# A decode layer on one Trainium2 core: the order of the loads, wo, w1 and w3 in single transfers, K transposed in place, one exp per row

## The chip, the cores and the metric

The kernel runs on one core of one Trainium2 chip. The metric is the device time of one execution in microseconds (us). Inputs and weights lie in HBM in bf16; every weight and the used part of the K and V caches are read once, 55.58 MB in all.

## The reference, cut to what matters

```python
# B=4, Sq=1, D=1024, Hq=32, Hkv=4, Sk=8192, Dh=128, F=3584; W = 2048 (the last keys)
h  = x + attention(layernorm(x))
    # q = layernorm(x) @ wq ; k, v = last W rows of the caches, each shared by 8 heads
    # p = softmax(q k^T * Dh**-0.5) ; attention = (p v) @ wo
h2 = h + (silu(n @ w1) * (n @ w3)) @ w2        # n = layernorm(h)
```

Four tokens, one per batch entry, pass through one attention block and one gated feed-forward block. There is little arithmetic per byte: each weight multiplies four rows.

## The kernel before

The kernel is written as a straight sequence. The scheduler of the framework is switched off (`tc.manual_schedule()`), so each engine executes its instructions in the order in which the code writes them: TensorE (PE) the matmuls and transposes, VectorE (DVE) and ScalarE (ACT) the copies, reductions and the exp, GpSimd (POOL) constants. SyncE (SP) issues all weight and cache loads, in the order of the list `ring` (L106), and an issue that has to wait holds back all that are behind it.

**Loads.** `stream` has five slots of 32 KB per partition. `fill()` (L118) issues the next part of `ring` as soon as the slot used five parts earlier has been given back by `done(...)`. The order is: the first half of wq, K in two pairs of batches, two slots that are reserved for the transposed K (kT, no load), the second half of wq, V in two pairs, wo in two pairs (four loads), w1 in two halves, w3 in two halves, w2 in six pieces of 7, 6, 8, 4, 2 and 1 rows per partition (L107). The pieces shrink so that little work is left after the last landing.

**Attention.** x comes in by four small loads on ACT's queue (L149), is transposed (L225) and normalised (`layernorm_T`, L192). The first half of wq is multiplied (L244, four strips of 32 array columns at once). Then K is transposed by PE in 32 steps of eight 128x128 blocks into PSUM (L264), and DVE and ACT in turn copy each step out to kT (L266, L268). The second half of wq follows, then q is copied, transposed (L278) and placed into Qm (L284). Scores are computed batch by batch (L299). For each batch there is a row maximum (`row_max`, L310), a bias by matmul, four exps (L339), each for one group g of heads: the bias of the other groups' rows is -1e30, so that each exp writes the probabilities of its own group and zeros elsewhere, interleaved by g. DVE transposes the result in 32x32 blocks (`transpose_p`, L349), and `output` (L358) multiplies with V (L374), scales by the inverse row sum and a mask (L383), and adds the four parts (L391). Eight small matmuls (L414), a copy, a DVE transpose and another copy bring the result into the layout oP.

**After attention.** wo is multiplied in 128 matmuls of 256 columns in four strips (L439); x is added by DVE (L449), the second layernorm follows, then w1 (L463), the gate silu (L477 to L481, with a reciprocal of 896 elements), w3, the product (L485), a transpose, and w2 (L496) piece by piece. Four small stores end the kernel.

Of the kernel before, what the change touches and what calls it, by code (L numbers as in the profile page):

```python
# [10 lines left out]
P = 128  # L11
# [6 lines left out]
NSLOT = 5  # L18
SLOT = 16384
NEG = -1.0e30  # L20
# [3 lines left out]
def kernel(  # L24
# [32 lines left out]
    C = 4  # L57
# [12 lines left out]
    T = REP  # L70
    L5 = 8
    JR = W // R
    JB = 8
    JM = 4
    wo_v = A_wo.rearrange("(g p t) n -> p g (t n)", g=Hkv, t=T)
# [8 lines left out]
    stream = ctx.enter_context(tc.tile_pool(name="stream", bufs=NSLOT))  # L84
# [4 lines left out]
    def of_cache(cache, b):  # L89
        return cache[b, :, Sk - W : Sk, :].rearrange("g (i j) d -> i g (j d)", j=JR)  # L90

    def pair(parts):
        return [parts[0:2], parts[2:4]]

    k_, v_ = (
        pair([(name, b, [JR, Dh], of_cache(cache, b)) for b in range(B)])
        for name, cache in (("k", A_k_cache), ("v", A_v_cache))
    )
    kT_ = pair([("kT", b, [JR, P], None) for b in range(B)])
    wo_ = pair([("wo", g, [1, T * D], wo_v[:, g : g + 1, :]) for g in range(Hkv)])  # L100

    def four_rows(name, view, n):
        return [[(name, i, [4, n], view[:, 4 * i : 4 * i + 4, :])] for i in range(KC // 4)]

    wq_ = four_rows("wq", wq_v, NQ)
    ring = wq_[:1] + k_ + kT_ + wq_[1:] + v_ + wo_ + four_rows("w1", w1_v, F) + four_rows("w3", w3_v, F)  # L106
    W2B = [7, 6, 8, 4, 2, 1]  # L107
    w2_ = []
    f0 = 0
    for i, n in enumerate(W2B):  # L110
        w2_.append(("w2", i, [n, D], w2_v[:, f0 : f0 + n, :]))
        f0 += n
    ring += [w2_[:2], w2_[2:]]
    views = {}
    taken = []
    used = set()

    def fill():  # L118

        while len(taken) < len(ring):  # L120
            n = len(taken) - NSLOT
            if n >= 0 and not all((name, i) in used for name, i, _, _ in ring[n]):
                break
            parts = ring[len(taken)]
            slot = stream.tile([P, SLOT], BF16, tag="slot", name="s_" + parts[0][0])
            o = 0
            for name, i, shape, src in parts:
                dst = slot[:, o : o + int(np.prod(shape))]
                o += int(np.prod(shape))
                view = dst.rearrange("p (a b) -> p a b", a=shape[0])  # L130
                if src is not None:
                    nc.sync.dma_start(out=dst if name in ("k", "v") else view, in_=src)  # L132
                views[(name, i)] = view
            taken.append(slot)

    def get(name, i):
        return views[(name, i)]

    def done(name, i):
        used.add((name, i))  # L140
        fill()
# [5 lines left out]
    nc.vector.memset(x_nat[:], 0.0)  # L147
    for c in range(C):
        nc.scalar.dma_start(out=x_nat[R * c : R * c + B, :], in_=x_flat[:, c * DQ : (c + 1) * DQ])  # L149
    fill()  # L150
# [3 lines left out]
    ones_f = const.tile([P, P], FP32)  # L154
    nc.vector.memset(ones_f[:], 1.0)
    eps_t = const.tile([P, 1], FP32)
    nc.vector.memset(eps_t[:], eps)

    t32 = const.tile([P, R], FP32)
    nc.vector.tensor_reduce(  # L160
        out=t32[:], in_=ident[:].rearrange("p (q h) -> p h q", q=C), axis=AX.X, op=ALU.add
    )
    ident_f = const.tile([P, P], FP32)
    nc.gpsimd.tensor_copy(out=ident_f[:], in_=ident[:])
    same = const.tile([P, C, R], FP32)
    for q in range(C):
        nc.gpsimd.tensor_copy(out=same[:, q], in_=t32[:])
    negm = const.tile([P, Hkv], FP32)
    nc.vector.tensor_reduce(
        out=negm[:], in_=t32[:].rearrange("p (g r) -> p g r", g=Hkv), axis=AX.X, op=ALU.add  # L170
    )
    nc.vector.tensor_scalar(
        out=negm[:], in0=negm[:], scalar1=-1.0, scalar2=-NEG, op0=ALU.add, op1=ALU.mult
    )
    jmask = const.tile([P, JM, 1], FP32)
    nc.vector.tensor_reduce(
        out=jmask[:, :, 0], in_=ident[:].rearrange("p (j h) -> p j h", j=JM), axis=AX.X, op=ALU.add
    )
    nscale = const.tile([P, Hkv], FP32)
    nc.vector.memset(nscale[:], -qscale)  # L180

    strip = const.tile([P, 2, P + B - 1], FP32)
    nc.gpsimd.memset(strip[:], 0.0)
    for l in range(2):
        nc.gpsimd.tensor_copy(
            out=strip[:, l, B - 1 :].rearrange("p (c x) -> p c x", c=C)[:, :, : B * Hkv].rearrange(
                "p c (g b) -> p c g b", b=B
            )[:, :, :, 0],
            in_=t32[:].rearrange("p (g c l) -> p l c g", g=Hkv, c=C)[:, l],
        )  # L190

    def layernorm_T(h_T, tag):  # L192

        both = act.tile([P, 2, KC, B], FP32, tag=tag + "_both")
        nc.vector.tensor_copy(out=both[:, 0], in_=h_T[:, :, :B])
        nc.vector.tensor_tensor(out=both[:, 1], in0=both[:, 0], in1=both[:, 0], op=ALU.mult)  # L196
        sums_ps = ps.tile([P, 2, KC, B], FP32, tag="kt3")
        nc.tensor.matmul(sums_ps[:], lhsT=ones_f[:], rhs=both[:], start=True, stop=True)  # L198
        sums = act.tile([P, 2, B], FP32, tag=tag + "_sums")
        nc.vector.tensor_reduce(  # L200
            out=sums[:], in_=sums_ps[:].rearrange("p t k b -> p t b k"), axis=AX.X, op=ALU.add
        )
        mean = act.tile([P, 2, B], FP32, tag=tag + "_mean")
        nc.vector.tensor_single_scalar(out=mean[:], in_=sums[:], scalar=1.0 / D, op=ALU.mult)
        rstd = act.tile([P, 1, B], FP32, tag=tag + "_rstd")
        nc.vector.tensor_tensor(out=rstd[:, 0], in0=mean[:, 0], in1=mean[:, 0], op=ALU.mult)
        nc.vector.tensor_tensor(out=rstd[:, 0], in0=mean[:, 1], in1=rstd[:, 0], op=ALU.subtract)  # L207
        nc.scalar.activation(  # L208
            out=rstd[:, 0], in_=rstd[:, 0], func=ACT.Sqrt, bias=eps_t[:], scale=1.0
        )  # L210
        nc.vector.reciprocal(out=rstd[:, 0], in_=rstd[:, 0])
        n_T = act.tile([P, KC, R], BF16, tag=tag + "_nT")
        nc.gpsimd.memset(n_T[:], 0.0)
        hc = act.tile([P, KC, B], FP32, tag=tag + "_hc")
        nc.vector.tensor_tensor(
            out=hc[:], in0=both[:, 0], in1=mean[:, 0:1, :].to_broadcast([P, KC, B]), op=ALU.subtract
        )
        nc.vector.tensor_tensor(
            out=n_T[:, :, :B], in0=hc[:], in1=rstd[:].to_broadcast([P, KC, B]), op=ALU.mult
        )  # L220
        return n_T
# [7 lines left out]
    x_T = act.tile([P, KC, R], BF16)  # L229
# [4 lines left out]
    q_ps = [ps.tile([P, REP // 2, Dh], FP32, tag=f"sc{hf}", name=f"q_ps{hf}") for hf in range(2)]  # L234
    HALF = REP // 2

    def query(i):
        w = get("wq", i)
        for kk in range(4):
            kc = 4 * i + kk  # L240
            for hf in range(2):
                for c in range(C):
                    o = (2 * c + hf) * HALF * Dh
                    nc.tensor.matmul(  # L244
                        q_ps[hf][R * c : R * c + R],
                        lhsT=xn_T[:, kc, :],
                        rhs=w[:, kk, o : o + HALF * Dh],
                        start=(kc == 0),
                        stop=(kc == KC - 1),
                        tile_position=(0, R * c),  # L250
                    )
        done("wq", i)

    query(0)


    n_step = 0
    for b in range(B):
        k = get("k", b)
        kT = get("kT", b)  # L260
        for jb in range(JR // JB):
            kt_ps = ps.tile([P, JB, P], BF16, tag=f"kt{n_step % 3}")
            for jj in range(JB):
                nc.tensor.transpose(out=kt_ps[:, jj], in_=k[:, jb * JB + jj, :], identity=ident[:])  # L264
            if n_step % 2 == 0:
                nc.vector.tensor_copy(out=kT[:, jb * JB : (jb + 1) * JB], in_=kt_ps[:])  # L266
            else:
                nc.scalar.copy(out=kT[:, jb * JB : (jb + 1) * JB], in_=kt_ps[:])  # L268
            n_step += 1
        done("k", b)  # L270

    query(1)
    q_sb = act.tile([P, REP, Dh], BF16)
    nc.vector.tensor_copy(out=q_sb[:, :HALF], in_=q_ps[0][:])
    nc.scalar.copy(out=q_sb[:, HALF:], in_=q_ps[1][:])
    qT_ps = ps.tile([P, REP, Hkv, R], BF16, tag="kt0")
# [6 lines left out]
    for b in range(B):  # L283
        nc.vector.tensor_copy(  # L284
            out=Qm[:, b].rearrange("p (g y) -> p g y", y=QW)[:, :, :REP],
            in_=qT_ps[:, :, :, b].rearrange("p r g -> p g r"),
        )


    sc_ps = [ps.tile([P, W // C], FP32, tag=f"sc{b}", name=f"sc_ps{b}") for b in range(B)]  # L290
# [4 lines left out]
    def scores(b, gs):  # L295
# [11 lines left out]
        if Hkv - 1 in gs:  # L307
            done("kT", b)
# [234 lines left out]
```

## Time and profile before

| | |
|---|---|
| time, median of 3 runs | 139.3 us (139.28 to 139.4) |
| the profiled execution's own time | 139.33 us |
| its span from the first to the last instruction | 137.5 us |
| mean granted TensorE clock | 0.812 |
| HBM read | 55.58 MB, 404 GB/s over the span |
| instructions | 2022 |

How to read the lines of the profile: a group names its source line, the engine, the operation, the tiles written and read, the shapes (partitions x elements, type) and the count; after the bar come its busy us and the mean ns of one; after the second bar the idle time of that engine just before, and what ended it. PEld is the weight load of TensorE, which overlaps with PE. In the 40 slices each entry stands for 3.44 us. PEclk is the clock that was granted to TensorE as a share of full speed. The chain of waits follows the work that ended last back from the last instruction.

### The profile page before, as it was taken

Reading aid. Unit: us, or ns where it says so; the run is one execution under the profiler, and the core shown is the slowest. Engines: PE = TensorE matmul, PEld = TensorE weight load, DVE = VectorE, ACT = ScalarE, POOL = GpSimd, SP = SyncE. Lnnn points to the kernel's source line nnn. Section 1 sums busy time; section 2 is a strip of 40 time slices with the busy share of each in tenths; the row PEclk is TensorE's granted clock in tenths of the full one; section 3 lists DMA queues with packets and bytes.
Section 4 is the critical chain, followed back from the end, with each engine's and each line's share of the span. In section 5 each row is a group of like instructions: output and inputs, shape, how many; then the busy total and the mean of one; then the engine's idle time right before and its main releaser. Section 6 shows DMA issues by size and latency. Waiting matters only on the chain.

```text
span 137.5 us, 2022 instructions
## 1 busy us (share of the span) xinstructions
PE 78.7 (57%) x866; PEld 45.4 (33%) x868; DVE 52.6 (38%) x97; ACT 42.7 (31%) x57; POOL 4.2 (3%) x18
## 2 busy tenths in 40 slices
PE   0000299999903889328936997948539600834271
PEld 0000139898801422114303353536424300322240
DVE  3001505666700235187165359551330596160001
ACT  1200006989820325998803940000040200000000
POOL 7400000000000000000000000000000000000000
PEclk9999999999995599955595599995995995595555
DMA  5998999999899999999999999999999999999950
GB/s 152 458 459 382 429 434 434 415 438 505 376 410 429 415 438 419 434 429 415 443 417 429 422 467 425 438 417 434 425 430 425 425 447 388 414 437 431 400 219 2
DMA packets 3529, 55.72 MB, mean 405 GB/s; under 512 B 416, under 2 KB 448, under 8 KB 704
## 3 DMA queue, kind: packets, MB, share of 16 engines
q1 hardware_dynamic: 3472, 55.58, 95.2%
q8 instruction: 7, 0.11, 0.3%
q10 hardware_dynamic: 48, 0.01, 0.0%
q14 instruction: 2, 0.02, 0.0%
HBM read 55.58 MB, written 0.01 MB: 404 GB/s over the span
## 4 chain that ended last, share of the span: by engine, by line
DMA 51%; PE 28%; DVE 13%; ACT 4%; issue 2%; SPq 1%; DVEq 0%
DMA s_wq<-in_A_wq_dram 31%; DMA s_w<-in_B_w_dram 20%; PE o_ps L374 11%; ACT P L339 4%; PE y_ps L439 4%; PE sc_ps L299 3%; DVE PT L351 3%; PE q_ps L244 2%; DVE om L391 2%; PE gu_ps L463 2%; DVE od L383 2%; PE tot_ps L360 1%; PE nm_ps L328 1%; PE on_ps L414 1%; SPq L132 1%
## 5 line engine op out<-in xcount | busy, mean ns | idle before, releaser
L339 ACT ACTIVATE P<-sc_ps,bias 128x512 bf16<-128x512 f32 x16 | 19.7, 1421 | 10.8 <-DVE bias L336 10.8
L374 PE MATMUL o_ps<-s_v,PT 128*128 128x512 bf16 x62 | 18.4, 457 | 0.3 <-issue 0.2
L268 ACT COPY s_kT<-kt_ps 128x1024 bf16<-128x1024 bf16 x16 | 15.6, 1012 | 6.8 <-PE kt_ps L264 6.8
L264 PE MATMUL kt_ps<-ident,s_k 128*128 128x128 bf16 x256 | 16.1, 219 | 1.1 <-ACT s_kT L268 1.0
L264 PEld LDWEIGHTS <-s_k 128*128 128x128 bf16 x256 | 15.0, 98 | 2.9 <-issue 2.5
L463 PE MATMUL gu_ps<-s_w,n_T 128*32 128x448 bf16 x128 | 9.8, 474 | 9.8 <-DMA s_w<-in_B_w_dram 8.0
L266 DVE COPY s_kT<-kt_ps 128x1024 bf16<-128x1024 bf16 x16 | 11.1, 692 | 10.1 <-PE kt_ps L264 10.1
L244 PE MATMUL q_ps<-s_wq,n_T 128*32 128x512 bf16 x64 | 7.2, 630 | 7.4 <-DMA s_wq<-in_A_wq_dram 5.6
L496 PE MATMUL y_ps<-s_w,hg_T 128*32 128x256 bf16 x112 | 6.6, 386 | 7.9 <-DMA s_w<-in_B_w_dram 5.3
L374 PEld LDWEIGHTS <-PT 128*128 128x128 bf16 x64 | 7.6, 123 | 9.8 <-issue 5.5
L208 ACT ACTIVATE rstd<-rstd,eps_t 128x4 f32<-128x4 f32 x2 | 0.6, 297 | 32.4 <-DVE rstd L207 32.4
L198 PE MATMUL sums_ps<-both,ones_f 128*128 128x64 f32 x4 | 1.1, 374 | 16.1 <-DVE both L196 16.1
L351 DVE STREAM_TRANSPOSE PT<-P 128x2048 bf16<-128x2048 bf16 x4 | 9.2, 2304 | 2.7 <-ACT P L339 2.7
L463 PEld LDWEIGHTS <-n_T 128*32 128x32 bf16 x128 | 4.4, 122 | 14.5 <-issue 11.5
L299 PE MATMUL sc_ps<-s_kT,Qm 128*32 128x512 bf16 x64 | 8.5, 603 | 0.4 <-DVE Qm L284 0.4
L496 PEld LDWEIGHTS <-hg_T 128*32 128x32 bf16 x112 | 4.2, 124 | 10.8 <-issue 6.8
L383 DVE SCALAR_TENSOR_TENSOR od<-o_ps,rinv,jmask 128x512 f32<-128x512 f32 x4 | 3.0, 750 | 9.4 <-PE o_ps L374 9.3
L198 PEld LDWEIGHTS sums_ps<-both,ones_f 128*128 128x128 f32 x4 | 0.8, 250 | 16.4 <-DVE both L196 16.4
L315 PE MATMUL mx_ps<-ident_f,rmax 128*1 128x128 f32 x8 | 1.9, 333 | 7.4 <-DVE rmax L313 7.4
L244 PEld LDWEIGHTS <-n_T 128*32 128x32 bf16 x64 | 2.4, 139 | 10.8 <-issue 8.6
L479 DVE RECIPROCAL eg<-eg 128x896 f32<-128x896 f32 x1 | 5.8, 5753 | 0.0
L439 PE MATMUL y_ps<-s_wo,oP 128*32 128x256 bf16 x128 | 4.9, 326 | 1.5 <-DVE oP L427 1.5
(68 smaller groups left out, 59.7 us busy)
## 6 DMA issues: line engine op xcount, KB each, us to landing
s_w<-in_B_w_dram SPq DMA_DIRECT2D x4, 3584.0 KB
s_wq<-in_A_wq_dram SPq DMA_DIRECT2D x2, 4096.0 KB, 12.3
s_k<-in_A_k_cache_dram SPq DMA_DIRECT2D x4, 2048.0 KB, 20.5
s_v<-in_A_v_cache_dram SPq DMA_DIRECT2D x4, 2048.0 KB
s_wo<-in_A_wo_dram SPq DMA_DIRECT2D x4, 2048.0 KB, 25.1
s_w<-in_B_w_dram SPq DMA_DIRECT2D x1, 2048.0 KB, 24.7
s_w<-in_B_w_dram SPq DMA_DIRECT2D x1, 1792.0 KB
s_w<-in_B_w_dram SPq DMA_DIRECT2D x1, 1536.0 KB
```

Of the source, the lines that this page charges most:

```text
L244: nc.tensor.matmul(q_ps[hf][R * c : R * c + R], lhsT=xn_T[:, kc, :], rhs=w[:, kk, o : o + HALF * Dh], start=(kc == 0), stop=(kc == KC - 1) ...
L264: nc.tensor.transpose(out=kt_ps[:, jj], in_=k[:, jb * JB + jj, :], identity=ident[:])
L266: nc.vector.tensor_copy(out=kT[:, jb * JB : (jb + 1) * JB], in_=kt_ps[:])
L268: nc.scalar.copy(out=kT[:, jb * JB : (jb + 1) * JB], in_=kt_ps[:])
L299: nc.tensor.matmul(sc_ps[b][R * q : R * q + R], lhsT=Qm[:, b, g * R : (g + 1) * R], rhs=v[:, g, q], start=(g == 0), stop=(g == Hkv - 1), t ...
L339: nc.scalar.activation(out=P4[:, :, :, g], in_=sc_ps[b][:].rearrange("p (j i) -> p j i", i=L5), func=ACT.Exp, bias=bias[:, g : g + 1], sca ...
L351: nc.vector.transpose(out=PT[:].rearrange("p j h -> p (j h)"), in_=stage.pop(("P4", b))[:].rearrange("p j i g -> p (j i g)"),)
L374: nc.tensor.matmul(o_ps[:], lhsT=PT[:, i * JM : (i + 1) * JM, :].rearrange("p j h -> p (j h)"), rhs=v[:, i * JM : (i + 1) * JM, :], start= ...
L439: nc.tensor.matmul(y_ps[R * c : R * c + R, :], lhsT=oP[:, g, t, :], rhs=w[:, 0, o : o + DQ], start=(g == 0 and t == 0), stop=(g == Hkv - 1 ...
L463: nc.tensor.matmul(out_ps[hf][R * c : R * c + R], lhsT=hn_T[:, kc, :], rhs=w[:, kk, o : o + FH], start=(kc == 0), stop=(kc == KC - 1), til ...
L479: nc.vector.reciprocal(out=eg[:], in_=eg[:])
L496: nc.tensor.matmul(y2_ps[R * c : R * c + R, :], lhsT=hg_T[:, fc, :], rhs=w[:, ff, c * DQ : (c + 1) * DQ], start=(fc == 0), stop=(fc == FC ...
```

## The change

- **Loads.** The ring of slots becomes one tile `ring` of five units of 32 KB per partition, and each matrix has a fixed place: wq in units 0 and 1, V of batches 0 and 1 in unit 2, K in units 3 and 4, V of batches 2 and 3 in unit 0, wo in units 3 and 4, w1 from unit 1, w3 from unit 3, w2's first 13 rows in unit 0 and the rest in unit 1. The order is now wq (one row of 8 KB per partition, then seven rows, 56 KB), K, V, wo in one load of 64 KB per partition, w1 and w3 in one load of 56 KB each, w2 in five pieces (13, 8, 4, 2, 1). Each load stands in the code behind the last reader of the place that it fills.
- **K.** A step has 16 blocks instead of 8, and its copy goes back to where the blocks came from (`transpose_k`). The scores of batches 0 and 1 stand between the transposes; those of batches 2 and 3 come after all of them. Batches 0 and 1 have three PSUM buffers for the steps, batches 2 and 3 have two.
- **Softmax.** Maximum and bias are computed for two batches at once. There is one exp per batch, written densely (`softmax`); DVE then multiplies it with a group mask into the interleaved layout (`spread`).
- **Output.** The four parts are added by POOL in two steps; four small matmuls (`place`) and one ACT copy bring the result into oP. x is added to wo's product by four matmuls with the identity, and wo's product itself is 64 matmuls of 512 columns in two strips.
- **Small steps.** Several constants, two steps of the layernorm's variance and its subtraction go from DVE to POOL; its copy and square to ACT; the gate's +1 from DVE to ACT. The products of w1 and w3 each go into one PSUM tile and are read in one instruction each.

The diff's core:

```diff
-    ring = wq_[:1] + k_ + kT_ + wq_[1:] + v_ + wo_ + four_rows("w1", w1_v, F) + four_rows("w3", w3_v, F)
-    W2B = [7, 6, 8, 4, 2, 1]
+    ring = stream.tile([P, 5 * UNIT], BF16)
+    wq_s = at(0, KC, NQ)
+    k_s = at(3, B, JR, Dh)
+    v_s = [at((2, 0)[b // 2], 2, JR, Dh)[:, b % 2] for b in range(B)]
+    wo_s = at(3, T, D)
+    w1_s = at(1, KC, F)
+    w3_s = at(3, KC, F)
+    W2B = [13, 8, 4, 2, 1]
...
+    for r in (slice(0, 1), slice(1, KC)):
+        load(wq_s[:, r, :], wq_v[:, r, :])
+    for b in range(B):
+        load(k_s[:, b].rearrange("p j d -> p (j d)"), k_v[:, :, b])
+    load_values(0)
...
+    load_values(1)                       # behind the query's matmuls
+    nc.scalar.copy(out=q_sb[:], in_=q_ps[:].rearrange("p a r d -> p (a r) d"))
...
+    def transpose_k(b, tags):
+        for n in range(JR // JB):        # JB = 16
+            blocks = k_s[:, b, n * JB : (n + 1) * JB, :]
+            kt_ps = ps.tile([P, JB, P], BF16, tag=tags[n_step % len(tags)], name="kt_ps")
+            for jj in range(JB):
+                nc.tensor.transpose(out=kt_ps[:, jj], in_=blocks[:, jj, :], identity=ident[:])
+            if n_step % 2 == 0:
+                nc.vector.tensor_copy(out=blocks, in_=kt_ps[:])
+            else:
+                nc.scalar.copy(out=blocks, in_=kt_ps[:])
+            n_step += 1
...
+    def spread(b):
+        nc.vector.tensor_tensor(
+            out=P4[:],
+            in0=stage.pop(("p1", b))[:].rearrange("p (x o) -> p x o", o=1).to_broadcast([P, JR * L5, Hkv]),
+            in1=gmask[:].to_broadcast([P, JR * L5, Hkv]),
+            op=ALU.mult,
+        )
...
+    transpose_k(0, ("ktA", "ktB", "scB"))
+    scores_tile(0)
+    scores(0, GS)
+    transpose_k(1, ("ktA", "ktB", "scB"))
+    scores(1, GS)
+    small = ps.tile([P, 2, 512], FP32, tag="ktB")
+    row_max(0)
+    transpose_k(2, ("ktA", "scB"))
+    bias_of(0)
+    softmax(0)
+    softmax(1)
+    spread(0)
+    transpose_k(3, ("ktA", "scB"))
+    scores_tile(1)
+    scores(2, GS)
+    scores(3, GS)
+    load(wo_s, wo_v.rearrange("p (t n) -> p t n", t=T))
+    transpose_p(0)
+    row_max(1)
+    spread(1)
+    bias_of(1)
+    softmax(2)
+    softmax(3)
+    transpose_p(1)
+    total(0)
+    output(0)
+    spread(2)
+    transpose_p(2)
+    output(1)
+    load(w1_s, w1_v)
+    spread(3)
+    transpose_p(3)
+    total(1)
+    output(2)
+    output(3)
...
+    for t in range(T):                   # T = 32
+        row = wo_s[:, t].rearrange("p (k i n) -> p i k n", k=2, i=2)
+        for i in range(2):
+            nc.tensor.matmul(
+                y_ps[R * i : R * i + R], lhsT=oP[:, t, :], rhs=row[:, i],
+                start=False, stop=(t == T - 1), tile_position=(0, R * i), skip_group_check=True,
+            )
+    load(w3_s, w3_v)
+    load(w2_s[0], w2_v[:, : W2B[0], :])
...
+    up_projection(w1_s, gate_ps)
+    for w, n in zip(w2_s[1:], W2B[1:]):
+        load(w, w2_v[:, fc : fc + n, :])
```

## The prediction

> **What bounds the kernel now.** I read the page's engine shares first, then the rate in the 40 slices, then busy time by stage (windows), then the chain of waits.
>
> ```profile
> span 137.5 us, 2022 instructions
> PE 78.7 (57%) x866; PEld 45.4 (33%) x868; DVE 52.6 (38%) x97; ACT 42.7 (31%) x57; POOL 4.2 (3%) x18
> GB/s 152 458 459 382 429 434 434 415 438 505 376 410 429 415 438 419 434 429 415 443 417 429 422 467 425 438 417 434 425 430 425 425 447 388 414 437 431 400 219 2
> q1 hardware_dynamic: 3472, 55.58, 95.2%
> DMA 51%; PE 28%; DVE 13%; ACT 4%; issue 2%; SPq 1%; DVEq 0%
> ```
>
> No engine is busy for more than 57% of the span, but the one load queue is busy for 95%, and no slice between the ramp at the start and the end falls away. The kernel is a stream of 55.58 MB at about 430 GB/s (129.3 us). The first six slices (20.6 us) moved 7.95 MB, which at 430 GB/s takes 18.5 us: the stream acts as if it began at 2.1 us, 1.4 us after its first issue at 0.73. It would end at 131.4; another 6.1 us pass to the end (engines that finish later, the last products, the store). So only two things matter: does a load always stand in the queue, and how long is the tail. The chain's PE and DVE parts are compute that runs beside the stream.
>
> Prices come from these groups and stretches (mean ns after the comma; in the last three rows PE's and DVE's busy us come third and fifth, PEclk and GB/s last):
>
> ```profile
> L268 ACT COPY s_kT<-kt_ps 128x1024 bf16<-128x1024 bf16 x16 | 15.6, 1012 | 6.8 <-PE kt_ps L264 6.8
> L266 DVE COPY s_kT<-kt_ps 128x1024 bf16<-128x1024 bf16 x16 | 11.1, 692 | 10.1 <-PE kt_ps L264 10.1
> L275 ACT CAST q_sb<-q_ps 128x512 bf16<-128x512 f32 x1 | 0.6, 586 | 8.2 <-PE q_ps L244 8.2
> L481 DVE TENSOR_TENSOR eg<-gu_ps,eg 128x448 f32<-128x448 f32 x2 | 1.2, 620 | 0.1
> L351 DVE STREAM_TRANSPOSE PT<-P 128x2048 bf16<-128x2048 bf16 x4 | 9.2, 2304 | 2.7 <-ACT P L339 2.7
> L339 ACT ACT_TABLE_LOAD x1 | 1.3, 1283 | 0.0
> 43.39 3.60 PE L244 MATMUL q_ps<-s_wq,n_T 128*32 128x512 bf16 x32 [5.60 <-DMA s_wq<-in_A_wq_dram]
> 35.79 2.00 PE L264 MATMUL kt_ps<-ident,s_k 128*128 128x128 bf16 x32 [0.16 <-ACT s_kT L268]
> 90.00:92.50 2.50, 1.38 (x10) 1.19 (x10) 0.99 (x3) 0.00 (x0) 0.00 (x0) 1.00 1.03 436
> 92.50:95.00 2.50, 1.58 (x32) 1.20 (x36) 0.77 (x2) 0.00 (x0) 0.00 (x0) 0.51 0.96 413
> 95.00:97.50 2.50, 2.50 (x84) 2.13 (x80) 0.00 (x0) 0.00 (x0) 0.00 (x0) 0.81 1.04 447
> ```
>
> **Part 1, fewer and longer transfers.** The bytes are the same. The trace's packets take 612 ns for 16 KB, 1066 for 28 and 1214 for 32, so each carries about 9 ns besides its bytes. Each of the 16 engines is spared 24 packets of wo, 8 of w1, 8 of w3 and 8 of w2 (six pieces become five): 48 x 9 ns = -0.4 us. 56 and 64 KB packets are not in the trace; between 32 KB's rate and none of this gain, 0 to -0.5. The store, the last load (one w2 row) and its products are the same, so the tail stays.
>
> **Part 2, the deadline that wo gets.** Before, wo took two slots as kT's were released one by one, and its four loads were issued from 47.0 to 53.1 us. Now wo_s covers exactly k_s (units 3 and 4), so its single load waits in SP's queue for the last scores matmul of batch 3. Ahead of it stand wq, K and V, 25.17 MB: 2.1 + 58.5 = 60.7 us. With 1.4 us from issue to rate, wo must be issued by 59.3. Behind it in SP's queue stand w1, w3 and w2, so each us late is a us of empty queue for everybody. The loads ahead of it are safe: V's second half waits for the query products (28.4 below) and is due at 2.1 + 48.8 - 1.4 = 49.5.
>
> **Part 3, when the scores end.** I follow the written order on each engine.
> - wq has landed at 2.1 + 19.5 + 1.2 (the chain has the first wq landing at 13.05, that much after 2.1 + 9.75) = 22.8. The x rows alternate with SP's packets as before, and layernorm takes about 3.6 us after them (13.35 to 17.0 now), so it is ready by then; the constants and three layernorm steps that go to POOL and two that go to ACT cost a few tenths under the same cover. Were all four x loads stuck between 56 KB packets, the cover would be gone and it would be 2 us late.
> - Query: row 0 is done; 14 groups of four remain. 8 groups took 3.60 us at half clock: 6.2 us, some 5.6 if the clock rises underway: 28.4. Then q_sb in one ACT copy (1.0, as for 1024 in L268), eight transposes (1.0), one Qm copy (0.35), handoffs: 30.9. K0's first chunk reuses qT's buffer and waits for it.
> - A chunk is now 16 transposes: 32 took 2.00 with a stop, 56 ns each at full clock, so 0.9, or 1.7 at half. ACT's eviction of 2048: 586 to 1012 ns for 512 to 1024 is 0.83 ns per element, so 1.86; DVE's 1.25 (159 ns + 0.52 per element, from L266 and the fixed part of L481). K0: four chunks 4.5 (first one at half clock), and ACT's second eviction ends 6.6 after the start: 37.5. scores(0) holds PE 1.7 (four groups of 0.43, as now). K1: 5.8 more; scores(1) 1.7 + 0.6 drain: 47.3. These eviction tails were hidden before, since scores came long after the last transpose.
> - row_max(0) stands ahead of K2 in PE's order: a reduce of 1024 (1.2, twice L313's 0.68 less the fixed part), the small matmul 0.4: K2 starts at 49.1. It has two buffers; the ACT one paces: two chunks, eviction, last chunk, eviction: 55.8.
> - ACT then loads the exp table (1.28, at that place in its order), and one exp: a plain 448 took 0.54 and the read of the sum is 0.29, so 0.9 (up to 1.4, L339's): 58.0. spread(0) on DVE, 2048 products: L481 gives 1.04 ns per element, 2.3; L266's bf16 rate would give 1.2. The change puts two broadcast operands in it, nearest to L481: 60.3.
> - K3's first eviction on DVE is queued behind that spread: 61.6. The third and fourth chunks wait for its buffer: 1.8 to 3.4, then ACT's last eviction 1.9, scores(2) and (3) 3.4 + 0.6. **The wo load is issued at about 70** (69.5 to 71).
>
> So the queue is empty for 70 - 59.3 = 10.7 us. Engines that ran ahead of the slowest meet again in that pause (the last slices fall to 219 GB/s over a full slice), worth some 0.5 us at the end.
>
> [...]
>
> The clock rows above: PE fell to half clock at 92.5 with 1.38 us of work in the 2.5 before, in two bursts. By the sums above the K stage has PE at 47 to 75% with pauses of 1 to 2.5 us, so I count half clock for some chunks (1.6 us in K3, 0.9 in K0). [...]
>
> **Part 4, what comes after.** One exp per row saves ACT 12 of 16 (about 1.2 apart: 14 us), all beside the stream. DVE gains four spreads (9.2) and loses the om sums (4.2) to POOL, at 0.3 to 1.1 per add. Both chains wait on DVE: from scores(3) at 70.6, reduce, small matmul, qmax, spread and bias (4.9), output(0) (5), od + spread + transpose for batches 2 and 3 (10.6), output(3) (3.5 to 5), od, adds, on, oP (3): about 99. w1 is issued after output(1) at about 85, and wo lasts until 91: in time. wo's product now uses two of four column strips: 4.9 us before, 32 pairs of 0.216 or 0.427 now, 7 to 13.7; y ends at 106 to 113. w3 waits for it; wo and w1 last until 71.4 + 36.6 = 108, so w3 is due at 106.6: late by 0 to 6. With the first 3.4 us at half clock, as after the gap at 92.5 now, the product takes 8.6: I take 1. The second layernorm, w1's product and the gate (its 5.75 us reciprocal) lie under w3 and the first w2 piece, 25 us of stream; the last four w2 pieces wait for w1's product, at about 118, and are due at 132.
>
> **Sum.** Profiled run 139.33 = span 137.5 + 1.83 around it; the median of the three runs is 139.3. Span: 137.5 - 0.4 + 10.7 - 0.5 + 1 = 148.3, minus 0.6 for the middle of the clock and spread bounds: 147.7; time 149.5.
>
> **Rivals.**
> - *The queue never runs dry* (faster). If scores(3) ends by 59.3, only -0.4 remains: 138.9. For: K has landed by 43, and PE's own work on K and scores is 14.4 + 6.8 us, which from 30.9 ends at 52. It decides at 59.3: 11 us of waits would have to vanish. Against: every wait above follows from an order written out. 5%.
> - *A short stall.* Full clock throughout, spread at the bf16 rate, table load hidden, evictions cheaper by 0.2 each: 70 - 2.5 - 1.1 - 1.3 - 0.5 = 64.6 and up to 1 earlier, so 3.8 to 5.3 us of empty queue on 139.33 - 0.9: 142.2 to 143.7. 10%.
> - *Two stalls.* PE at half clock through K1 to K3 (8 chunks, half of it exposed: +3) and through wo's product (+6): 154 to 158. For: the clock slices show 0.5 after each pause; against: the product follows output(3) directly, and warmed up in 2.5 us at 95. 12%.
> - *Nothing visible*, gain and a small stall cancelling (wo at 60 to 60.5): 2%.
>
> **How the numbers follow.** The forecast case, wo late by 6 to 13 us, holds 71%; with 0 to 2 us for w3 it spans 144 to 153.5. The range 142.5 to 154 adds the near ends of its two neighbours. 0.2% (0.28 us) is about what a measurement can tell: faster 0.05, same 0.02, slower 0.93.
>
> **What would show it.** In the profile after: a hole in GB/s from about 61 to 71 us; SP waiting for PE's scores before wo's issue; a wo product starting on DMA or on output, and y's matmuls at about 7 to 9 us; DVE's eviction of K3's third step right behind a 2.3 us TENSOR_TENSOR; ACT evictions of 1.86. An unbroken stream with wo issued before 59 makes the forecast wrong as a whole; an ACT eviction under 1.5 or full PE clock from 30 to 70 shrinks it.

## The result, and the profile after

The changed kernel takes 152.1 us (median of six runs, 151.25 to 152.66), against 139.42 for the kernel before on the same chip (six runs, 139.28 to 139.51). The ratio is 1.090, 95% interval 1.086 to 1.095: 12.7 us slower. The profiled run is the highest of the six, 152.66 us, with a span of 150.9. The medians and ranges of the experiments are those of fast runs, so one slow run of e2 (153.65 us) and one of e4 (148.58 us) are left out of them.

The page of the kernel after, its engine shares, its rate in 40 slices of 3.77 us, the load queue, and the engines' shares of the chain:

```profile
span 150.9 us, 1801 instructions
PE 75.9 (50%) x786; PEld 42.8 (28%) x788; DVE 48.6 (32%) x45; ACT 28.4 (19%) x31; POOL 15.0 (10%) x39
GB/s 185 581 472 258 487 378 417 421 447 434 426 417 417 421 443 430 52 0 278 278 556 278 556 324 441 476 487 426 289 471 476 395 350 413 424 404 413 319 24 4
q1 hardware_dynamic: 2608, 55.58, 87.0%
PE 33%; DMA 32%; DVE 13%; ACT 11%; issue 5%; POOL 2%; ACTq 0%; POOLq 0%; DVEq 0%
```

The same 55.58 MB are moved, and every engine but POOL is busy for less time than before. But slices 17 and 18 hold 52 and 0 GB/s, the queue's share falls from 95.2 to 87.0%, and the chain now runs through compute: DMA holds 32% of it instead of 51. (The 278s and 556s behind the hole are not a slow stream: a 64 KB packet takes 2.42 us, and its bytes are booked in one slice. The whole stretch from 73 to 107 us gives 432.)

The hole by stretches of 2.5 us (after the length: PE, PEld, DVE, ACT, POOL busy us, PEclk, DMA share, GB/s):

```profile
60.00:62.50 2.50, 2.16 (x21) 2.16 (x21) 0.54 (x2) 0.00 (x0) 0.00 (x0) 0.50 0.37 151
62.50:65.00 2.50, 1.41 (x14) 1.25 (x12) 2.50 (x2) 1.05 (x1) 0.00 (x0) 0.71 0.00 0
65.00:67.50 2.50, 1.63 (x16) 0.49 (x19) 0.69 (x1) 0.82 (x1) 0.00 (x0) 1.00 0.00 0
67.50:70.00 2.50, 1.99 (x20) 0.38 (x12) 0.47 (x1) 0.00 (x0) 0.00 (x0) 1.00 0.00 0
```

Most of the 16 DMA engines finish V's last packets at about 60.9 (two only at 62.3 and 62.7), wo is issued at 69.56 and its packets begin at 70.54: 9.6 us with nothing in the queue for most of them. What ran meanwhile stands in the chain of the kernel after (start, length, what):

```profile
54.76 1.28 ACT L324
...
56.90 2.17 issue
59.07 1.23 DVE ring L262
...
60.34 3.58 PE kt_ps L260 x32
63.95 1.87 ACT ring L264
65.87 3.65 PE sc_ps L283 x27
```

This is the written order, read off: behind ACT's last eviction of K2 come the exp table and the exp; the 2.17 us called issue is DVE in spread(0) (56.86 to 59.16). Only then comes DVE's eviction for K3, two chunks of K3 that had waited for its buffer, ACT's eviction, and the scores of batches 2 and 3. SP's own waits name what each of the late loads stood behind (total us, times, longest):

```profile
SPq L123 <- PE y_ps L460: 14.5, 1, 14.5
SPq L123 <- PE small L374: 11.5, 1, 11.5
...
SPq L123 <- PE sc_ps L283: 6.0, 1, 6.0
```

They are, in this order, w3 behind wo's product (issued at 105.78), w1 behind output(1) (81.49) and wo behind the scores (69.56). Only the last left the whole queue empty: w1's last packets land between 107.7 and 109.6, after w3 is already queued. (By a narrow margin: two engines had finished w1 by 107.84 and got their first packets of w3 only at 109.42 and 109.47; neither is the one whose w3 lands last.) The priced groups:

```profile
L264 ACT COPY ring<-kt_ps 128x2048 bf16<-128x2048 bf16 x8 | 14.8, 1866 | 19.7 <-PE kt_ps L260 19.7
L262 DVE COPY ring<-kt_ps 128x2048 bf16<-128x2048 bf16 x8 | 9.8, 1224 | 11.5 <-PE kt_ps L260 11.5
L337 DVE TENSOR_TENSOR P<-p,gmask 128x2048 bf16<-128x2048 bf16 x4 | 9.1, 2280 | 3.5 <-ACT p L324 3.5
L391 POOL TENSOR_TENSOR o<-od 128x256 f32<-128x256 f32 x4 | 6.8, 1695 | 64.6 <-DVE od L382 64.6
L460 PE MATMUL y_ps<-ring,oP 128*32 128x512 bf16 x64 | 8.8, 443 | 0.1
```

**Where the 13.4 us of span are.** The first DMA engine to finish has its last landing at 142.51 instead of 132.14: +10.4. The last engine follows 3.6 us later instead of 1.9: +1.75. From the last landing to the end it takes 4.7 us instead of 3.5: +1.25. The +10.4 is the 9.6 us of empty queue, plus 0.5 to 1.0 for wo's first packets (2.9 to 3.4 us instead of 2.42), less the spared packets.

### The profile page after: what moved, and what is told of

The parts are those of the page before. It is cut to its first block, busy times and chain, and to the rows that moved or that the text cites. A ratio compares the mean times of both kernels' runs of the same rounds, so it can differ in the third digit from the quotient of the medians.

```text
span 150.9 us, 1801 instructions
## 1 busy us (share of the span) xinstructions
PE 75.9 (50%) x786; PEld 42.8 (28%) x788; DVE 48.6 (32%) x45; ACT 28.4 (19%) x31; POOL 15.0 (10%) x39
## 3 DMA queue, kind: packets, MB, share of 16 engines
q1 hardware_dynamic: 2608, 55.58, 87.0%
HBM read 55.58 MB, written 0.01 MB: 368 GB/s over the span
## 4 chain that ended last, share of the span: by engine, by line
PE 33%; DMA 32%; DVE 13%; ACT 11%; issue 5%; POOL 2%; ACTq 0%; POOLq 0%; DVEq 0%
DMA ring<-in_B_w_dram 21%; DMA x_nat<-in_A_x_dram 10%; ACT ring L264 9%; PE kt_ps L260 8%; PE y_ps L460 6%; PE sc_ps L283 5%; DVE P L337 4%; PE q_ps L226 4%; PE o_ps L374 3%; PE small L374 2%; DVE PT L359 2%; PE gate L484 2%; DVE rmax L295 2%; DVE od L382 1%; ACT L324 1%
## 5 line engine op out<-in xcount | busy, mean ns | idle before, releaser
L260 PE MATMUL kt_ps<-ident,ring 128*128 128x128 bf16 x256 | 18.5, 240 | 6.5 <-DVE ring L262 4.9
L260 PEld LDWEIGHTS <-ring 128*128 128x128 bf16 x256 | 17.4, 109 | 8.2 <-issue 8.2
L264 ACT COPY ring<-kt_ps 128x2048 bf16<-128x2048 bf16 x8 | 14.8, 1866 | 19.7 <-PE kt_ps L260 19.7
L262 DVE COPY ring<-kt_ps 128x2048 bf16<-128x2048 bf16 x8 | 9.8, 1224 | 11.5 <-PE kt_ps L260 11.5
L391 POOL TENSOR_TENSOR o<-od 128x256 f32<-128x256 f32 x4 | 6.8, 1695 | 64.6 <-DVE od L382 64.6
L283 PE MATMUL sc_ps<-ring,Qm 128*32 128x512 bf16 x64 | 7.4, 604 | 5.9 <-ACT ring L264 5.9
L337 DVE TENSOR_TENSOR P<-p,gmask 128x2048 bf16<-128x2048 bf16 x4 | 9.1, 2280 | 3.5 <-ACT p L324 3.5
L460 PE MATMUL y_ps<-ring,oP 128*32 128x512 bf16 x64 | 8.8, 443 | 0.1
L374 PE MATMUL o_ps<-ring,PT 128*128 128x512 bf16 x31 | 8.4, 425 | 0.2 <-issue 0.2
L374 PE MATMUL small<-ring,PT 128*128 128x512 bf16 x31 | 7.2, 379 | 0.7 <-DVE rinv L355 0.7
```

Of the source, the lines that this page charges most:

```text
L260: nc.tensor.transpose(out=kt_ps[:, jj], in_=blocks[:, jj, :], identity=ident[:])
L262: nc.vector.tensor_copy(out=blocks, in_=kt_ps[:])
L264: nc.scalar.copy(out=blocks, in_=kt_ps[:])
L283: nc.tensor.matmul(sc_ps[b // 2][R * q : R * q + R, b % 2], lhsT=Qm[:, b, g * R : (g + 1) * R], rhs=kT[:, b, g, q], start=(g == 0), stop=( ...
L337: nc.vector.tensor_tensor(out=P4[:], in0=stage.pop(("p1", b))[:].rearrange("p (x o) -> p x o", o=1).to_broadcast([P, JR * L5, Hkv]), in1=g ...
L374: nc.tensor.matmul(o_ps, lhsT=PT[:, i * JM : (i + 1) * JM, :].rearrange("p j h -> p (j h)"), rhs=v_s[b][:, i * JM : (i + 1) * JM, :], star ...
```

## The experiments

The theory: the load queue is served in order, each of its loads has a deadline set by the loads ahead of it, and one late chain of compute misses the deadline of wo; the longer packets, K in place and the single exp cost nothing by themselves. The rivals: the changed compute, or the long transfers, are slower in themselves, or the hole is a small part and the rest comes from the wo, w1 and w3 products.

### e1: wo in two halves, the first behind scores(1)

```diff
     scores(1, GS)
+    load(wo_s[:, : T // 2], wo_v.rearrange("p (t n) -> p t n", t=T)[:, : T // 2])
...
     scores(3, GS)
-    load(wo_s, wo_v.rearrange("p (t n) -> p t n", t=T))
+    load(wo_s[:, T // 2 :], wo_v.rearrange("p (t n) -> p t n", t=T)[:, T // 2 :])
```

> wo comes in two halves of 32 KB per partition: the first is issued behind scores(1) (46 us in the profile after), the second where the whole was. The queue then does not run dry at 61 us. Theory (a row of deadlines, all set by the same late chain on DVE and PE): the pauses only move. w1 is still issued at 81.5, where the queue would now be dry at 80.4, and w3 still at 105.8, since wo's product waits for output(3) and not for wo. Gain 0.1 to 0.9 us: 151.2 to 152.0. Rival (wo's one wait costs the 9.6 us of empty queue): 142 to 143.

Measured: 150.07 us (149.08 to 150.45), ratio 1.075 (1.071 to 1.080). The first half is issued at 46.15, and the stream runs on. The rate of this kernel in 40 slices of 3.71 us:

```profile
GB/s 159 619 278 464 495 322 428 424 446 424 428 428 424 424 428 428 446 419 424 406 424 318 433 309 494 483 263 0 247 247 494 483 494 245 445 434 404 408 62 4
```

Slices 17 and 18 are full (446, 419), and the hole stands in slices 27 to 29 instead: w1 has landed at 100.2 to 101.7, and w3 is issued at 105.53, as in the kernel after (105.78). So curing one deadline alone moves the pause to the next: both are set by the same chain. That removes the rival by which the hole at wo is all there is. The gain of 2.0 us is larger than expected: the first engine's last landing is 0.85 earlier, and the engines end 2.1 us apart instead of 3.6.

### e2: the first spread computed twice

```diff
-        nc.vector.tensor_tensor(
+        for _ in range(times):
+            nc.vector.tensor_tensor(
...
-    spread(0)
+    spread(0, 2)
```

> spread(0) is executed twice (2.28 us more on DVE, same result), ahead of K3's first eviction. Theory: wo's issue and everything behind it move by that amount, one to one: 154.2 to 154.6. Rival (the loss lies in coarse landings or in the end of the stream, and DVE has room): less than 0.5 us more.

Measured: 152.03 us (150.95 to 152.99), ratio 1.091 (1.085 to 1.098): no more than the kernel after (152.1), with intervals that reach about 1 us to either side, and not 2.1 to 2.5 more. By the time alone this is what the rival had. The profiled run is its fastest. In it the first links hold: PE's pause ahead of K3 grows from 4.50 to 6.83 us, by the price of one spread, and since everything ahead of it came 0.6 earlier here, wo is issued at 71.25, 1.7 later than in the kernel after; the first engine's landing of wo is 1.76 later (92.52) and that of w1 1.76 (109.46). Of this, 1.16 is left at its last landing (143.67); where the other 0.6 went is open. And the engines end 1.8 us apart here, 3.6 in the kernel after, so that the last landing of all is even earlier (145.49 against 146.15), and two stores that were 1.05 late in the kernel after are not late here. So in this execution the doubled spread did pass into the stream, and the uneven end of the engines and the stores, which my expectation took as fixed, covers it. For the runs without a trace that is not shown. A difference of 1 to 2 us can't be read from the times of these kernels with a hole; the landings tell it.

### e3: all of K3's transposes ahead of the exp

```diff
     bias_of(0)
+    transpose_k(3, ("ktA", "scB"))
     softmax(0)
     softmax(1)
     spread(0)
-    transpose_k(3, ("ktA", "scB"))
```

> K3's transposes stand ahead of the first two exps and spread(0), so that K3's eviction on DVE no longer waits for the spread. Worked out from the rows of after: last eviction at 60.8, wo issued at 64.5 (69.6 before). spread(0) then comes at 62.9 to 65.1, its transpose until 67.4, row_max(1) at 67.4 instead of 69.5, so the chain behind and w3's issue gain only 2.1. Theory (row of deadlines): wo's pause shrinks by 5 us, a new one of 2 us opens ahead of w3, sum -2 to -3 us: 149.1 to 150.1. Rival (only wo's issue counts): -5: 147. Rival (coarse landings): no change.

Measured: 151.49 us (150.76 to 152.03), ratio 1.087 (1.083 to 1.091): a gain of 0.6, not 2 to 3. The place of the 4.5 us was right: wo is issued at 65.02. But the first exp came 6.5 us later (62.58 against 56.05), so that the second row maximum's product gained only 1.6 (69.20 against 70.81), and then two of the four output products ran at half clock. A stretch of this kernel, with 8 matmuls in 2.5 us; PEclk stands at 0.50, as it does from 68.0 to 78.3:

```profile
73.00:75.50 2.50, 2.50 (x8) 1.12 (x9) 2.10 (x2) 1.31 (x4) 0.00 (x0) 0.50 0.97 419
```

These two took 6.0 and 6.6 us instead of 5.1 and 3.6, w3 was issued 1.7 later (107.44), and a gap opened ahead of it, since w1 had landed between 103.15 and 105.38. Again one deadline was paid with the next. The clock had a part of chance in it: the second fall came behind a pause of PE of 2.6 us (82.82 to 85.45), and the like pause in the kernel after (83.18 to 85.81) left the clock at full.

### e4: the loads alone moved, none of the compute

wo and w1 are split in halves, and 20 rows of w2 go ahead of w3 into places that are free sooner:

```diff
-    W2B = [13, 8, 4, 2, 1]
+    W2B = [16, 4, 5, 2, 1]
...
     scores(1, GS)
+    load(wo_s[:, : T // 2], wo_v.rearrange("p (t n) -> p t n", t=T)[:, : T // 2])
+    load(w1_s[:, : KC // 2], w1_v[:, : KC // 2])
...
     output(1)
-    load(w1_s, w1_v)
+    load(w1_s[:, KC // 2 :], w1_v[:, KC // 2 :])
...
     output(3)
+    load(w2_s[0], w2_v[:, : W2B[0], :])
+    load(w2_s[1], w2_v[:, W2B[0] : W2B[0] + W2B[1], :])
...
     load(w3_s, w3_v)
-    load(w2_s[0], w2_v[:, : W2B[0], :])
```

> Only loads are moved and split, no engine does other work: wo's first half behind scores(1), w1's first half (unit 1 has been free since the query) behind it, then the second halves where the wholes were; 16 rows of w2 in unit 0 and 4 in the free end of unit 2 ahead of w3; the last 8 rows in three pieces. Theory: every issue comes before the queue is dry (wo's second half at 69.6, due 77.6; w1's at 81.5, due 87.3; w2 at 93, due 95.9; w3 at 105.8, due 108.1), so the stream is unbroken: 139.0 to 140.5. Rival (K in place, long packets, PE's half clock or the spreads cost by themselves): above 145.

Measured: 147.78 us (146.06 to 148.02), ratio 1.057 (1.051 to 1.064). The half that concerns the stream held: it is unbroken, with its last landing at 134.05 (before: 134.02). The time missed the expected range by 7.3 us, for a reason that I had put there myself. The end of this kernel's chain:

```profile
129.08 5.07 PE up L487 x57
...
134.18 1.10 DVE hg L511
...
135.30 1.71 DVE hg_T L211
...
137.06 4.52 PE small L524 x96
```

w3 now lands at 129.04, and w3's product, the gate, a transpose and the whole product of w2 follow it: 12.5 us of compute that had lain under w2's loads. The order of the loads sets two things, when each place must be free and what is left to compute when the last byte is there.

### f1: the same, but all of w3 ahead of w2

w3 is split in halves too; its first goes to unit 0 behind the outputs, its second to unit 3 behind the first half of wo's product, and w2 stays last:

```diff
-    w3_s = at(3, KC, F)
-    W2B = [13, 8, 4, 2, 1]
+    w3_s = [at(unit, KC // 2, F) for unit in (0, 3)]
+    W2B = [16, 5, 4, 2, 1]
...
     output(3)
+    load(w3_s[0], w3_v[:, : KC // 2])
...
+        if t == T // 2 - 1:
+            load(w3_s[1], w3_v[:, KC // 2 :])
-    load(w3_s, w3_v)
```

> As e4, but w3 stands ahead of w2 in the stream again: its first half in unit 0 behind output(3), its second in unit 3 as soon as the first half of wo's product has been read, then 16 rows of w2 in unit 4 behind wo's product and 12 in unit 1 behind w1's. In e4 the stream was unbroken (last landing 134.05 us, before 134.02), but w3 landed at 129 and 13 us of products followed. Theory (the loss is the order of deadlines; long packets, K in place, one exp and the spreads cost nothing by themselves): last landing about 134, w3 at 117, gate done at 124 to 126, w2's rows waited for as before: 139.0 to 141.0. Rival (the later compute is a bound of its own): w3's product and w2 end 3 us or more behind the landing: 142 or more.

Measured: 140.42 us (140.08 to 140.67), ratio 1.0074 (1.0055 to 1.0093), as expected. The rate in 40 slices of 3.46 us has no hole, and only the engines' uneven end at the last:

```profile
GB/s 159 477 464 531 266 530 317 445 450 403 436 440 407 421 455 402 431 526 355 407 429 497 421 452 379 416 481 402 406 439 464 406 414 445 455 369 411 404 79 5
```

K in place, the dense exp, the spread and the POOL adds are all still there: 11.7 of the 12.7 us were the order and size of four loads. That refutes the rival by which the changed compute is slow in itself. For the long transfers the evidence is another, since f1 has wo, w1 and w3 in halves again: one packet took 2.42 us for 64 KB and 2.12 for 56, against 1.21 for 32 and 1.07 for 28, so that a byte is no slower in them.

### f2: f1, with wo's product in four strips again

```diff
-    y_ps = ps.tile([2 * R, 2, DQ], FP32, tag="ktA")
+    y_ps = ps.tile([P, DQ], FP32, tag="ktA")
...
-        for i in range(2):
+        for c in range(C):
             nc.tensor.matmul(
-                y_ps[R * i : R * i + R],
+                y_ps[R * c : R * c + R, :],
```

> f1 with wo's product in four strips of 256 columns as before the change (128 matmuls, x added by four identity matmuls). Theory: wo's product 4.9 us instead of 7 to 8.8, so the second layernorm, w1 and the gate come 2 to 4 us earlier and the end is set by the last landing alone: 138.6 to 139.8, f1 minus 0 to 1.2. If f1 already ends with the landing, no difference.

Measured: 139.75 us (139.71 to 140.01), ratio 1.0031 (1.0018 to 1.0044). wo's product takes 3.7 us (98.75 to 102.43) against 7.1 in f1 and 8.8 in the kernel after. This version is the best with the changed compute, and still 0.3% behind the kernel before. That the strips made it faster than f1 is not shown: the stores are issued at 134.93 here and already at 134.60 in f1 (134.97 in the kernel before), and what makes f1's span longer, 138.4 against 138.0, is two stores that come 1.0 us late there (see the last section). Its last landing (133.99) and its result (134.9) stand where they stood before; its span is 0.5 longer behind the landing of the stores, and what these 0.5 us are stays open.

### f3: the kernel before, with only wo held back

A write of one element by ACT, from the scores of batch 3, into wo's place makes its load wait:

```diff
+            if parts[0][0] == "wo" and ("kT", B - 1) not in used:
+                break
...
+                if name == "wo" and o == int(np.prod(shape)):
+                    nc.scalar.copy(out=slot[:1, :1], in_=sc_ps[B - 1][:1, :1])
```

> The kernel before with one part of the change alone: both wo slots are written with one element of the last scores by ACT ahead of the load, so that wo waits for scores(3) there too (about 63.1 us: ACT has first to finish the exps of batch 1). Due at 59.3, so a pause of 3.8 and 0.4 for the restart; all later loads have 8 us or more of slack. Theory: 142.7 to 143.8. Rival (a pause in the queue is made up for later): 139.3 to 140.

Measured: 143.15 us (142.71 to 143.6), ratio 1.027 (1.024 to 1.030). wo is issued at 62.94, 3.6 us after the deadline of 59.3 that the prediction worked out; the last landing moves by 3.53 us (137.55) and the time by 3.8. Here, where every deadline behind has slack, the one-to-one step does hold. A late wo alone makes the old kernel slow, with none of the new compute in it.

### f4: the kernel before, with only the dense exp and the spread

```diff
-        for g in range(Hkv):
-            nc.scalar.activation(
-                out=P4[:, :, :, g],
...
+        nc.scalar.activation(
+            out=p1[:],
+            in_=sc_ps[b][:],
...
+        nc.vector.tensor_tensor(
+            out=P4[:].rearrange("p j i g -> p (j i) g"),
+            in0=p1[:].rearrange("p (x o) -> p x o", o=1).to_broadcast([P, JR * L5, Hkv]),
+            in1=gmask[:].to_broadcast([P, JR * L5, Hkv]),
+            op=ALU.mult,
+        )
```

> The kernel before with the softmax of the change alone: one dense exp per row and the spread on DVE, no other part. ACT is spared 14 us, DVE gets 9. Theory: the stream is unbroken in both and the softmax lies beside it: 139.0 to 139.6. Rival (ACT's exps hold up the kernel before): faster by 1 us or more; rival (DVE becomes the bound): slower by 1 us or more.

Measured: 139.37 us (139.19 to 139.56), ratio 1.0001 (0.9991 to 1.0010). The 16 exps of the kernel before, and the two groups of f4 that replace them:

```profile
L339 ACT ACTIVATE P<-sc_ps,bias 128x512 bf16<-128x512 f32 x16 | 19.7, 1421 | 10.8 <-DVE bias L336 10.8
```

```profile
L345 DVE TENSOR_TENSOR P<-p,gmask 128x2048 bf16<-128x2048 bf16 x4 | 9.2, 2292 | 3.5 <-ACT p L337 3.5
L337 ACT ACTIVATE p<-sc_ps,bias 128x512 bf16<-128x512 f32 x4 | 2.7, 687 | 25.8 <-DVE bias L334 25.8
```

ACT's busy time falls from 42.7 to 26.0 us and DVE's rises from 52.6 to 60.8. Neither shows in the time, since both lie beside an unbroken stream.

## Why the prediction was right, and which terms were off

The forecast case came: slower by a hole ahead of wo, 152.1 against 149.5 us, inside the range of 142.5 to 154.

- **The deadline** (59.3 us) holds. V's last packets ended at 60.9 on most engines, where the sum had 60.7, and f3 shows the price of missing it: 3.6 us late, 3.5 us at the last landing.
- **The chain of the scores** holds step by step, each 1.1 to 1.3 us earlier than worked out: T0 at 29.84 (30.9), scores(1) done at 46.23 (47.3), K2 evicted at 54.7 (55.8), exp done at 56.74 (58.0), spread done at 59.16 (60.3), DVE's eviction at 60.29 (61.6). The lead was made early: wq landed at 22.49 (22.8), its 14 groups took 5.2 us (5.6), and the way from there to T0 2.2 (2.5). The layernorm's cover was nearly gone, since x landed at 18.05 and the query began at 21.70, 0.8 ahead of wq's landing. The 0.9 us of half clock in K0 did not come (32 transposes took 1.96). wo was issued at 69.56 ("about 70"): part of the lead was given back, since the scores of a batch took 1.9 us where the sum had 1.7. K3's half clock cost 1.67 (32 transposes in 3.58 against 1.91; 1.6 counted).
- **The prices** hold: ACT's eviction 1866 ns (1.86 us), DVE's 1224 (1.25), the spread 2280 (2.3), the exp 0.78 us with the read of its sum (0.9, the near side), wo's product 8.8 us (8.6).
- **The stall**: 9.6 us of empty queue and 0.5 to 1.0 for first packets, against 10.7.
- **"Engines meet again in that pause, -0.5" failed**, in sign. The engines' last landings lie 3.6 us apart instead of 1.9: +1.75. They do meet at wo (its landings lie 0.5 apart), but the distance is made behind it. At w1's landing one engine is 1.4 us behind the other fifteen (109.63 against 108.21), at w3's 1.6 behind the next (128.93 against 127.31). Two instruction fetches of 16 KB lie ahead of these, at 94.9 and 116.5, of 0.96 and 0.93 us. The trace doesn't name the engines, but packets that follow one another without a gap put both on one: from the first fetch, which ends at 95.87, six packets run to 109.30, the last of w1; three of w3 run from 109.37 to 116.47, then comes the second fetch, and five more run from 117.38 to 128.47, the last of w3. In e2, with the like two at 96.6 and 117.9, the engines end 1.8 apart. I had no term for that.
- **"The tail stays" failed** in this execution: +1.25. The final result comes 0.92 us after the last landing in both kernels; then two of the four stores have a packet that lands 1.05 us behind the rest (149.68 and 149.86, the others by 148.82). What goes with it stands in the last section.
- **w3 "late by 1" failed**: 0 on the first engine and on the one whose w3 lands last. It was issued at 105.78, and w1 landed only at 107.7; two other engines stood without a packet for 1.6 us or more there. With the hole at wo everything behind it had that much more time.
- **-0.4 for packets**: the fastest engine ends at 132.01 in f1 and 131.92 in f2, against 132.14 before, with some of the packets spared: 0.1 to 0.2. On the engine that ends last it is 0.25 in f1 (133.77 against 134.02) and nothing in f2 (133.99).

So the sum of 147.7 was 3.2 us short of the span. The three failed terms explain 1.25 + 1.75 + 0.5 - 1.0 = 2.5 of it; the rest is that the first engine came 10.4 late where 10.7 - 0.4 - 0.6 = 9.7 was worked out.

The slow rate for the spread was my estimate, and it came out: 2280 ns for 2048 products here and 2292 in f4, where DVE's bf16 eviction of 2048 took 1224. Why it runs at that rate no run shows.

The half clock in K3 was counted from the row at 92.5 before and the work that the stage was to have. In the 4.5 us pause of PE from 55.84 to 60.34 the clock fell 1.3 us into the pause. The stretches at half clock that lie whole in the spans before and after last 3.41 us or a multiple of it (in the kernel before 92.53 to 95.94, in the kernel after 57.13 to 63.96, 74.20 to 77.61 and 98.09 to 101.51). The length of a pause alone does not tell these falls: in the kernel after and in e2 PE paused for the same 2.31 us ahead of the small products that make oP. The stretch that follows, of the kernel after and then of e2:

```profile
98.00:100.00 2.00, 2.00 (x12) 0.74 (x10) 0.00 (x0) 0.00 (x0) 0.00 (x0) 0.52 1.06 459
```

```profile
98.00:100.00 2.00, 1.55 (x14) 1.15 (x16) 0.00 (x0) 0.27 (x1) 0.31 (x1) 1.00 0.99 430
```

The clock fell to half in one and stayed full in the other, and wo's product took 8.8 us in the one and 7.1 in the other; what decides between them is not shown. It cost little here, since w1 was still landing when w3 was issued; in e3 half clock did cost.

## What to carry to other kernels

A kernel that streams through one load queue in order is a row of deadlines: for each load, the bytes ahead of it say when it must be issued, and the last reader of its place says when it can be. Merging transfers and giving each matrix a fixed place moves the second time later for all behind it, so work out both for every load before trading places or sizes, and remember that curing one late load exposes the next. Put last in the queue what leaves the least compute behind it, and expect no gain from faster compute that lies beside an unbroken stream (f4: 139.37 us against 139.39).

## What the hardware showed that was not expected

**An add on POOL takes 2.7 us beside a spread, and 0.72 alone.** From the timeline of the kernel after:

```profile
80.44 2.28 DVE L337 TENSOR_TENSOR P<-p,gmask 128x2048 bf16<-128x2048 bf16 x1
80.60 2.70 POOL L391 TENSOR_TENSOR o<-od 128x256 f32<-128x256 f32 x1 [57.88 <-DVE od L382]
...
94.96 0.72 POOL L391 TENSOR_TENSOR o<-od 128x256 f32<-128x256 f32 x1 [2.38 <-DVE od L382]
```

The first add starts 0.16 us behind the spread and ends 0.58 behind its end, as if it did its work only then; the second, 2.63 us long, ends 0.58 behind its spread too. The last, with no spread beside it, takes 0.72. The price of 0.3 to 1.1 us was right for the second case alone. Why the add takes longer beside a spread is not shown. Here it cost nothing, since the outputs waited for PE and DVE.

**Small loads on another queue pay for long packets.** x's four loads on ACT's queue landed at 13.2 us between packets of 32 KB and at 18.05 between packets of 56 KB (4.8, 9.4, 13.7 and 18.05). Each of these loads shows as packets of 512 B and then of 4 B, and from the second load on each of the two stands behind a big packet: in the second they begin at 6.6 to 6.9 and at 8.8 to 9.1, one packet of 56 KB (2.12 us) apart.

**One instruction fetch among the stores goes with 1 us at the end.** The page of the kernel after counts the fetches (packets, MB, share):

```profile
q8 instruction: 6, 0.10, 0.3%
q14 instruction: 1, 0.01, 0.0%
```

The one of q14, 8 KB, begins at 148.29, in the middle of the stores (147.10 to 148.8), and two of the stores have their late packet. In the ten profiles of this study it falls among the stores five times (the kernel after, e1, e3, e4 and f1), and those five have packets 0.9 to 1.2 us late; in the other five it falls elsewhere (in e2 at 130.3, in the kernel before at 69.7 and 78.2), and no store is late. The late packets begin where the fetch ends: in the kernel after it ends at 148.71, and the last packet of two stores begins at 148.71 and 148.74, 0.4 to 0.5 behind the others of its store; the other four show the same. The late stores go with the fetch in ten of ten; moving it was not tried.
